# First keys of an attention kernel loaded in two pieces a head and transposed in two pieces

## The chip, the cores and the metric

The kernel runs on one core of a Trainium2 chip. The metric is the time of one execution on the device, in microseconds (us), as a median of several runs. The core has five engines, each with an instruction queue of its own that runs in order: PE (TensorE, matmuls and transposes; PEld is its loading of weights), DVE (VectorE), ACT (ScalarE), POOL (GpSimd) and SP (SyncE, which here only issues transfers). Transfers between the chip's memory (HBM) and the core's (SBUF) are issued by SP, ACT or POOL and carried by 16 DMA engines. Matmul results land in PSUM, from which DVE or ACT copy them.

## The reference

Causal attention with 16 extra "beacon" keys and values ahead of each head's own, then a two-layer network with a leaky ReLU on the joined heads. B = 8 batches, H = 8 heads, S = 576 positions, head size D = 64, 16 beacons; 4608 tokens of width 512, inner width 2048. All inputs and the output are float32.

```python
k_all = np.concatenate([beacon_k, k], axis=2)
v_all = np.concatenate([beacon_v, v], axis=2)
scores = scale * np.matmul(q, k_all.transpose(0, 1, 3, 2))
scores = np.where(causal, -1000000000.0, scores)      # beacons are never masked
a = softmax(scores)
attn_out = np.matmul(a, v_all)
x = attn_out.transpose(0, 2, 1, 3).reshape(B * S, H * D)
h = x @ w_in
out = np.maximum(0.01 * h, h) @ w_out
```

## The kernel before

**Tiling.** Heads are worked on in pairs: group g is batch g // 4, pair g % 4, so there are 32 groups. The two heads of a pair lie on partitions 0 to 63 and 64 to 127 of a transposed operand (head size on partitions, positions in columns). Keys of a group stand in `kT`: 16 beacon columns, then 576 keys. `score(g, n)` (s0.0 to s0.3 for group 0) multiplies blocks of 128 key columns with the queries: s0.0 uses key columns 0 to 127 (beacons and keys 0 to 111), s0.1 the next 128, s0.2 and s0.3 the rest. Each is followed by an exponential on ACT (L276) into `aT`, and POOL masks the triangles (`mask`, L289). `value(g, half)` multiplies the masked exponentials with V (L359). After that `up` and `down` steps do the two layers (L442, L544), which fill PE for the rest of the run.

**How a position lies in a loaded tile.** A load of queries or keys is read as "(p i) d": row p of 64 partitions holds the nine consecutive positions 9p to 9p + 8, so that a row of float32 is 9 x 64 x 4 = 2304 bytes. PE transposes one i of the nine at a time, and the copy out of PSUM puts position 9p + i into column 9p + i.

**Loads.** Queries and keys of the first eight groups are loaded by POOL with a cast to bfloat16 (`load_qk`, L158); V by POOL too (`load_v_cast`, L209 and L214). The keys of group 0 alone go by SP without a cast (`load_first_keys`, L163): two transfers, one a head, each of 64 rows to partitions 0 to 63 of two buffers `first_k`, which share their memory with the tiles `gsum2` (the profile calls them gsum). The beacon keys of the first two batches go by ACT's queue (L185). After the cast of head 0 on ACT (L928) and head 1 on DVE (L929) both heads stand side by side in `k_nat0`, 64 partitions.

**Transposes of group 0.** `t_q(0, 0)` transposes the queries (18 transposes, L243) and ACT copies all 576 columns out (`q0.1`: engine 1 of the pair dve, act). `t_q(0, 1)` transposes the keys from `k_nat0`, nine transposes of 64 x 128 (L238), and DVE copies them in two parts: the first 13 rows of p (117 columns) and the rest (459 columns), L249.

**Order.** The order on every engine is written out by hand. A string of steps is read by `run`: s score, m mask, v value, q and k transposes with copies, l and V loads, i loads of the first layer's weights, w and W unused matmuls that write nothing that is read, and so on. Steps without a letter in `run` (the first keys, beacon casts and transposes, the making of constants) are called between the strings. In the head this is the order:

```python
        unused(13, 256)
        cast_beacon_k(0, 2, nc.scalar.copy)
        beacon_transposes(0, 2)
        unused(13)
        nc.scalar.copy(out=k_nat0[:, :, 0], in_=first_k[0])
        nc.vector.tensor_copy(out=k_nat0[:, :, 1], in_=first_k[1])
        run("q0.1 k0 w2.384 s0.0 m0.0 w3.256 s0.1 q1 s0.2 m0.1 k1 s0.3 m0.2")
```

An engine takes from this list the instructions that are its own, in this order. POOL's queue has all loads from l0.0 to i0 ahead of the first mask.

Of the kernel before, what the change touches and what calls it, by code (L numbers as in the profile page):

```python
# [8 lines left out]
FP32 = mybir.dt.float32  # L9
BF16 = mybir.dt.bfloat16  # L10
# [5 lines left out]
def kernel(  # L16
# [11 lines left out]
    nc = tc.nc  # L28

    B, H, S, D = q.shape  # L30
    NB = beacon_k.shape[2]
# [74 lines left out]
    def sum_tile(n):  # L106
        return sumpool.tile([128, NF * 128], BF16, name=f"gsum{n}")

    QK = 2 * RI * D
    first_k = [  # L110
        sum_tile(2)[0:RP, 0:QK].bitcast(FP32).rearrange("p (i d) -> p i d", i=RI) for _ in range(2)
    ]
    k_nat0 = singles.tile([RP, RI, 2, D], BF16, name="k_nat0")
    bk_raw = singles.tile([128, B, D], FP32, name="bk_raw")
    bk = singles.tile([128, B, D], BF16, name="bk")

    def make_pads():
        nc.vector.memset(k_all[:, :, NB + S :], 0.0)
        for t in a_bufs:
            for c in PADS:  # L120
                nc.vector.memset(t[:, :, c : c + 48], 0.0)

    def make_ones():
        for t in v_bufs:
            nc.vector.memset(t[:, :, :, D : D + 1], 1.0)
# [30 lines left out]
    def load_qk(g, which):  # L156
# [2 lines left out]
            out=raw_of(b, grp)[which][rows],  # L159
            in_=(q, k)[which][b, 2 * hp : 2 * hp + 2].rearrange("h (p i) d -> p h i d", i=RI),  # L160
        )

    def load_first_keys():  # L163
        for h in range(2):
            nc.sync.dma_start(out=first_k[h], in_=k[0, h].rearrange("(p i) d -> p i d", i=RI))

    def load_natural(g, which):
        b, hp = divmod(g, NPAIR)
# [15 lines left out]
    def load_beacon_k(b0, b1, eng):  # L184
        eng.dma_start(out=bk_raw[:, b0:b1], in_=beacon_k[b0:b1].rearrange("b h n d -> (h n) b d"))  # L185

    def cast_beacon_k(b0, b1, copy):
        copy(out=bk[:, b0:b1], in_=bk_raw[:, b0:b1])

    def beacon_transposes(b0, b1):  # L190
        ps = ps_one.tile([128, 1024], BF16, name="tp", tag="one")
        for b in range(b0, b1):
            for par in range(2):
                nc.tensor.transpose(
                    ps[par * 64 : par * 64 + 64, (b - b0) * 128 : (b - b0 + 1) * 128], bk[:, b], ident
                )
        for par in range(2):
            ps_ = slice(par * 64, par * 64 + 64)
            src = ps[ps_, 0 : (b1 - b0) * 128].rearrange("p (x e n) -> p e x n", e=2, n=NB)[:, par]
            if b0 == 0:  # L200
                nc.vector.tensor_copy(out=k_all[ps_, :, 0:NB], in_=src)
            else:
                nc.vector.tensor_copy(out=bkT[ps_, b0:b1].rearrange("p b h n -> p (b h) n"), in_=src)
# [15 lines left out]
    def operand(g, which):  # L219
        qk.setdefault(g, [None, None])  # L220
        if which == 0:
            qk[g][0] = headpool.tile([128, S], BF16, name="qT", bufs=5)
            return qk[g][0]
        qk[g][1] = k_bufs[g % NK]
        return qk[g][1][:, NB : NB + S]
# [5 lines left out]
    def t_q(g, which, copy):  # L231
        b, hp, grp, rows = where(g)
        dst = operand(g, which)
        ps = ps_one.tile([128, 1024], BF16, name="tp", tag="one")
        psv = ps[:, 0:S].rearrange("c (i p) -> c i p", i=RI)
        for i in range(RI):
            if (g, which) == (0, 1):
                nc.tensor.transpose(  # L238
                    psv[:, i], k_nat0[:, i].rearrange("p h d -> p (h d)"), ident[0:RP, 0:RP]
                )  # L240
                continue
            for par in range(2):
                nc.tensor.transpose(  # L243
                    psv[par * 64 : par * 64 + 64, i], qk_raw[b, grp][which][rows, par, i], ident[rows, rows]
                )
        cut = 13 if (g, which) == (0, 1) else RP
        for lo, hi, eng in ((0, cut, copy), (cut, RP, nc.vector.tensor_copy)):
            if lo < hi:
                eng(  # L249
                    out=dst.rearrange("c (p i) -> c p i", i=RI)[:, lo:hi],  # L250
                    in_=psv.rearrange("c i p -> c p i")[:, lo:hi],
                )

    probs = {}

# [206 lines left out]
    def weight_sums(part):  # L462
        b11, b12 = w_out_sb[:, 0:HF, 0:HD], w_out_sb[:, 0:HF, HD:DM]
        b21, b22 = w_out_sb[:, HF:NF, 0:HD], w_out_sb[:, HF:NF, HD:DM]
        t1, t2, t4 = (w_sum[:, i] for i in range(3))
        tt = nc.vector.tensor_tensor
        if part == 0:
            tt(out=t1, in0=b12, in1=b11, op=SUB)
            tt(out=t2, in0=b22, in1=t1, op=SUB)
            tt(out=t4, in0=b21, in1=t2, op=SUB)  # L470
        else:
            tt(out=b12, in0=b22, in1=b12, op=SUB)
# [348 lines left out]
    def unused(n, cols=128):  # L821
        ps = ps_one.tile([128, 512], FP32, name="av", tag="one")
        r, w = max(1, cols // 128), min(cols, 128)
        for i in range(n):
            nc.tensor.matmul(
                out=ps[:, 0 : r * w].rearrange("p (r w) -> p r w", w=w),
                lhsT=blank,
                rhs=blank[:, None, 0:w].to_broadcast([128, r, w]),
                start=True,
                stop=True,  # L830
            )

    def unused_ahead(g, half, n):
        if (g, half) not in avs:
            avs[g, half] = ps_one.tile([128, 512], FP32, name="av", tag="one")
        for i in range(n):
            nc.tensor.matmul(
                out=avs[g, half][:, 400:512], lhsT=blank, rhs=blank[:, 0:112], start=True, stop=True
            )

    NG = B * NPAIR
    KEPT, LEAD, LEFT = 4, 4, 14

# [16 lines left out]
    def run(steps):  # L860
        for step in steps.split():
            op, a = step[0], [int(x) for x in step[1:].split(".")] if step[1:] else []
            if op == "s":
                score(*a)
            elif op == "m":
                mask(*a)
            elif op == "v":
                value(*a)
            elif op == "e":
                value_ahead(*a)  # L870
            elif op == "x":
                finish(*a)
            elif op == "l":
                load_qk(*a)
            elif op == "V":
                load_v_cast(*a)
            elif op == "N":
                load_natural(*a)
            elif op == "T":
                turn_pair(a[0])  # L880
            elif op == "y":
                x_turn(a[0])
            elif op == "q" or op == "k":
                t_q(a[0], 0 if op == "q" else 1, (dve, act)[a[1] if len(a) > 1 else 0])
            elif op == "b":
                beacon_columns(a[0], (dve, act, pool)[a[1]])
            elif op == "u":
                up()
            elif op == "d":
                down()  # L890
            elif op == "w":
                unused(*a)
            elif op == "W":
                unused_ahead(*a)
            elif op == "i":
                load_w_in(a[0])
            elif op == "o":
                load_w_out(a[0])
            elif op == "t":
                weight_sums(a[0])  # L900
            else:
                raise ValueError(step)

# [8 lines left out]
        }  # L912
    )
    with order:
        load_first_keys()
        load_beacon_k(0, 2, nc.scalar)
        nc.vector.memset(blank, 0.0)
        nc.vector.memset(ident, 0.0)
        run("l0.0 l1.0")
        make_identity(nc, ident, nomemset=True)  # L920
        make_ones()
        run("l1.1 l2.0 l2.1 V0.0 V0.1 l3.0 l3.1 V0.2 V0.3 V0.4 l4.0 l4.1 i0")
        make_pads()
        unused(13, 256)
        cast_beacon_k(0, 2, nc.scalar.copy)
        beacon_transposes(0, 2)
        unused(13)
        nc.scalar.copy(out=k_nat0[:, :, 0], in_=first_k[0])  # L928
        nc.vector.tensor_copy(out=k_nat0[:, :, 1], in_=first_k[1])  # L929
        run("q0.1 k0 w2.384 s0.0 m0.0 w3.256 s0.1 q1 s0.2 m0.1 k1 s0.3 m0.2")  # L930
        run("w2.384 s1.0 m1.0 q2 s1.1 k2 w2.384 s1.2 m1.1 w2.384 s1.3 m1.2 W0.0.4 s2.0 m2.0 W0.0.4 s2.1 W0.0.6 q3 l5.0 l5.1 s2.2 k3 w4.384 v0.0 m2.1 s2.3 i1 m2.2 W0.1.4 s3.0 m3.0 v1.0 s3.1 v0.1 s3.2 v1.1 m3.1 l6.0 l6.1 s3.3 x0.1 m3.2")
        run("v2.0 V1.0 V1.1 q4 v2.1 x1 k4.1 v3.0 v3.1 x2.1 s4.0 s4.1 x3 m4.0 V1.2 V1.3 V1.4 l7.0 l7.1 u u s4.2 s4.3 q5 k5 m4.1 m4.2 u o0 u")
        load_beacon_k(2, B, nc.gpsimd)
        run("s5.0 s5.1 m5.0 u u u s5.2 s5.3 q6 k6 m5.1 m5.2 o1 u u s6.0 s6.1 m6.0 u v4.0 u v4.1 y4 N8.0 N8.1 u s6.2 s6.3 q7 k7 m6.1 m6.2 u")
        cast_beacon_k(2, B, nc.gpsimd.tensor_copy)
        run("u v5.0 u v5.1 N9.0 s7.0 s7.1 m7.0 d x5 v6.0 v6.1 T8 d s7.2 s7.3")
        beacon_transposes(2, B)
        run("m7.1 m7.2 N9.1 u b8.2 b9.2 b10.2 b11.2 x6 v7.0 T9 v7.1 d d d N10.0 N10.1 d V2.0 V2.1 x7 t0 T10")


        FIRST = 2 * NPAIR
        COLS = FLAT[NKB]
# [99 lines left out]
```

## Time and profile before

| | us |
|---|---|
| median of the runs | 324.58 |
| lowest and highest run | 324.3, 325.61 |
| span of the profiled execution | 323.8 |
| PE busy in the span | 314.3 |
| ACT busy | 203.8 |
| POOL busy | 184.3 |
| DVE busy | 168.0 |

The span is the time from the first to the last instruction of one profiled execution; of that execution no other time is given. A row of the timeline reads: start in us, length in us, engine, line of the kernel, operation, what is written and read, shapes, how many instructions were merged, and in brackets how long the engine stood idle before and which instruction or transfer ended that. A row of the groups has the count, the total busy time in us, the mean in ns and the idle time. A row of the stretches has the stretch, its length, and the busy time of PE, PEld, DVE, ACT and POOL. A row of the DMA queues has packets, MB and the time that the packets took as a share of all 16 engines over the stretch; queue 0 is POOL's, queue 1 SP's, queue 10 ACT's.

### The profile page before, as it was taken

The numbers are of one execution on the slowest core, as the hardware profiler recorded it, in microseconds if no ns is written. First come the engines' busy times: TensorE is split into PE (matmuls) and PEld (weight loads), VectorE is DVE, ScalarE is ACT, GpSimd is POOL, SyncE is SP. The second block draws the span as 40 slices with busy tenths as digits, with TensorE's granted clock in tenths as the row PEclk, the third lists the DMA queues.
The fourth block names the chain that finished last, engine by engine and source line by source line (L and its number), as shares of the span: only waits on it lengthen the run. The fifth ranks groups of instructions, "written<-read, shape, count | busy, mean of one in ns | idle before, by whom it ended". The sixth has DMA issues, their size and how long they took to land.

```text
span 323.8 us, 8701 instructions
## 1 busy us (share of the span) xinstructions
PE 314.3 (97%) x3468; PEld 219.1 (68%) x3494; DVE 168.0 (52%) x341; ACT 203.8 (63%) x346; POOL 184.3 (57%) x354
## 2 busy tenths in 40 slices
PE   7999999999999999999999999999999999999995
PEld 4575555444588557855788888656875697688784
DVE  3464245508255244444443454525464689577954
ACT  4968962387855786478746874687458547455510
POOL 8895868999996787659875977666221000000000
PEclk9999999999999999999999999999999999999999
DMA  8999999999999999999999999999222100200123
GB/s 137 129 189 192 124 214 140 169 177 188 135 152 160 216 138 129 114 186 97 141 176 174 99 143 119 188 128 129 44 81 82 26 2 32 75 25 2 65 67 130
DMA packets 155256, 39.78 MB, mean 123 GB/s; under 512 B 142368, under 2 KB 152480, under 8 KB 155216
## 3 DMA queue, kind: packets, MB, share of 16 engines
q0 software_dynamic: 99824, 18.54, 91.1%
q1 hardware_dynamic: 55120, 20.62, 38.3%
q8 instruction: 27, 0.44, 0.6%
q14 instruction: 13, 0.11, 0.1%
q10 hardware_dynamic: 272, 0.07, 0.1%
HBM read 37.22 MB, written 9.44 MB: 144 GB/s over the span
## 4 chain that ended last, share of the span: by engine, by line
PE 72%; DMA 14%; POOL 9%; ACT 3%; issue 1%; DVE 0%; POOLq 0%; ACTq 0%; SPq 0%
PE acc L442 24%; PE acc L544 19%; PE sc L544 11%; PE av L359 6%; PE sc L314 5%; PE acc L663 5%; DMA w_out_sb<-in_moe_w_out_dram 4%; DMA gsum<-in_k_dram 4%; POOL aT L289 3%; DMA k_nat<-in_k_dram 3%; DMA v_aug<-in_v_dram 2%; ACT aT L333 2%; DMA kT<-k_nat 2%; POOL gsum L158 1%; POOL v_aug L214 1%
## 5 line engine op out<-in xcount | busy, mean ns | idle before, releaser
L442 PE MATMUL acc<-xT,w_in_sb 128*128 128x512 bf16 (+1 forms) x537 | 116.5, 354 | 1.5 <-ACT aT L329 0.3
L450 ACT ACTIVATE gT<-acc 128x512 bf16<-128x512 f32 x124 | 70.8, 623 | 33.1 <-PE acc L442 32.6
L289 POOL TENSOR_SCALAR_AFFINE_SELECT aT<-aT 128x256 bf16<-128x256 bf16 (+2 forms) x160 | 59.7, 403 | 51.4 <-ACT aT L329 31.5
L442 PEld LDWEIGHTS <-w_in_sb 128*128 128x128 bf16 x560 | 51.7, 98 | 43.9 <-issue 2.9
L544 PEld LDWEIGHTS <-gT 128*128 128x128 bf16 x512 | 48.7, 98 | 7.7 <-issue 1.8
L333 ACT ACTIVATE aT<-sc 128x1024 bf16<-128x1024 f32 (+3 forms) x64 | 51.7, 892 | 0.0
L329 ACT ACTIVATE aT<-sc 128x512 bf16<-128x512 f32 (+3 forms) x64 | 29.0, 520 | 27.8 <-PE sc L314 27.8
L388 DVE RECIPROCAL rec<-av 128x6 f32<-128x6 f32 (+1 forms) x64 | 12.0, 187 | 65.0 <-PE av L359 64.4
L359 PEld LDWEIGHTS <-aT 128*128 128x128 bf16 (+1 forms) x960 | 36.9, 98 | 9.2 <-issue 1.4
L544 PEld LDWEIGHTS <-gsum 128*128 128x128 bf16 x384 | 36.5, 98 | 6.5 <-issue 0.4
L359 PE MATMUL av<-v_aug,aT 128*128 128x65 bf16 (+1 forms) x960 | 39.8, 194 | 0.8 <-DMA v_aug<-in_v_dram 0.4
L214 POOL DMA_DIRECT2D v_aug<-in_v_dram x40 | 34.1, 856 | 4.2 <-DMA w_in_sb<-in_moe_w_in_dram 3.8
L171 POOL DMA_DIRECT2D k_nat<-in_k_dram x48 | 34.8, 730 | 0.9 <-DMA w_out_sb<-in_moe_w_out_dram 0.3
L171 POOL DMA_DIRECT2D q_nat<-in_q_dram x48 | 34.8, 729 | 0.6 <-issue 0.4
L389 DVE TENSOR_TENSOR x_nat<-av,rec 128x384 bf16<-128x384 f32 (+1 forms) x64 | 31.4, 491 | 2.2
L544 PE MATMUL acc<-w_out_sb,gT 128*128 128x256 bf16 x240 | 28.9, 273 | 0.4 <-ACT gT L450 0.4
L276 ACT ACTIVATE aT<-sc 128x1024 bf16<-128x1024 f32 (+3 forms) x32 | 26.0, 874 | 4.7 <-PE sc L267 2.5
L314 PE MATMUL sc<-qT,kT 64*128 64x80 bf16 (+22 forms) x384 | 22.2, 250 | 0.3
L314 PEld LDWEIGHTS <-kT 64*128 64x128 bf16 x384 | 12.8, 94 | 11.2 <-issue 7.6
L544 PE MATMUL acc<-w_sum,gsum 128*128 128x256 bf16 x160 | 20.1, 273 | 0.0
L575 ACT COPY p<-acc 128x512 f32<-128x512 f32 x15 | 9.1, 604 | 16.8 <-PE acc L544 16.8
L785 DVE TENSOR_TENSOR gsum<-gT 128x1024 bf16<-128x1024 bf16 x16 | 11.0, 688 | 15.7 <-ACT gT L450 15.7
(95 smaller groups left out, 339.0 us busy)
## 6 DMA issues: line engine op xcount, KB each, us to landing
out_dram<-p SPq DMA_DIRECT2D x26, 256.0 KB, 3.2
q_nat<-in_q_dram POOLq DMA_DIRECT2D x48, 72.0 KB, 5.5
k_nat<-in_k_dram POOLq DMA_DIRECT2D x48, 72.0 KB, 5.3
v_aug<-in_v_dram POOLq DMA_DIRECT2D x24, 128.0 KB, 6.5
w_in_sb<-in_moe_w_in_dram POOLq DMA_DIRECT2D x2, 1024.0 KB, 12.4
w_out_sb<-in_moe_w_out_dram POOLq DMA_DIRECT2D x2, 1024.0 KB, 12.1
out_dram<-u SPq DMA_DIRECT2D x8, 256.0 KB, 2.7
gsum<-in_q_dram POOLq DMA_DIRECT2D x8, 144.0 KB, 7.1
```

The lines of the kernel that those rows point to most:

```text
L171: nc.gpsimd.dma_start(out=t[:, :, par], in_=(q, k)[which][b, 2 * hp + par].rearrange("(t p) d -> p t d", p=NR),)
L214: nc.gpsimd.dma_start(out=dst[lo : ROWS[c], c, :, 0:D], in_=v[b, :, OFF[c] : OFF[c] + n].rearrange("h p d -> p h d"),)
L276: nc.scalar.activation(out=aT[:, :, c0 : c0 + w], in_=sc[:, :, 0:w], func=AF.Exp, scale=0.125)
L289: nc.gpsimd.affine_select(out=view, in_=view, compare_op=ALU.is_ge, fill=0.0, base=128 - n if lo == 0 else 0, channel_multiplier=-1, patte ...
L314: nc.tensor.matmul(out=(sc[par] if apart else sc[:, par])[:, at : at + b - a], lhsT=kT[ps_, c * 128 : (c + 1) * 128], rhs=qT[ps_, q0 : q0 ...
L329: nc.scalar.activation(out=probs[g][:, par, lo:hi], in_=sc[par][:, at : at + hi - lo], func=AF.Exp, scale=0.125)
L333: nc.scalar.activation(out=probs[g][:, :, lo:hi], in_=sc[:, :, at : at + hi - lo], func=AF.Exp, scale=0.125)
L359: nc.tensor.matmul(out=avv[:, n, 0 : D + 1], lhsT=aT[0 : ROWS[c], par, a0 : a0 + 128], rhs=va[0 : ROWS[c], c, 2 * hp + par, :], start=(c = ...
L389: nc.vector.tensor_tensor(out=x_nat[:, t0:t1].rearrange("p t e d -> p (t e) d"), in0=avv[:, :, 0:D], in1=rec[:, n0:n1, None].to_broadcast( ...
L442: nc.tensor.matmul(out=acc[:, lo:hi], lhsT=w_in_cols(fc, j), rhs=xT[:, j, x0 : x0 + hi - lo], start=(j == 0), stop=(j == NJ - 1), skip_gro ...
L450: nc.scalar.activation(out=gT[i][:, fc, :], in_=acc, func=AF.Prelu, alpha=0.01)
L544: nc.tensor.matmul(out=acc[:, lo : lo + HD], lhsT=left(i, n, fc, tile), rhs=right(n, fc), start=(lo == 0 and fc == 0), stop=(fc == HF - 1) ...
```

## The change

The two heads' first keys now lie one below the other, head h on partitions 64h to 64h + 63 of one buffer `first_k`, and each head comes in two transfers on SP: rows 0 to 26 of p (keys 0 to 242), then rows 27 to 63. The order on SP is: both heads' first pieces (F0.0, F1.0), then both second pieces (F0.1, F1.1). The first pieces are cast by ACT (h0.1) and DVE (h1.0). `first_keys(0)` (g0.0) makes 18 transposes of 27 partitions each, and DVE copies 243 columns. After the scores s0.0 and s0.1, `first_keys(1)` (g1.0) makes 18 transposes of 64 partitions, and DVE copies the other 333 columns. Ahead of it H0, on DVE, casts the whole of `first_k`, 128 partitions x 576, into `k_nat0` at once; on DVE's queue it stands behind its part of the first queries' copy.

The copy of the first queries (q0.1) is split: ACT copies rows 0 to 31 of p (288 columns), DVE the other 288. The cast h1.0 stands on DVE ahead of the copies of the beacon transposes. There are 8 and 4 unused matmuls of 128 columns around g0.0 where there were 13 ahead of the casts. The rest of the order is as before; all of it is now one string, `HEAD`, with letters for what was called between the strings.

```diff
-    first_k = [
-        sum_tile(2)[0:RP, 0:QK].bitcast(FP32).rearrange("p (i d) -> p i d", i=RI) for _ in range(2)
-    ]
-    k_nat0 = singles.tile([RP, RI, 2, D], BF16, name="k_nat0")
+    first_k = sum_tile(2)[:, 0:QK].bitcast(FP32).rearrange("p (i d) -> p i d", i=RI)
+    k_nat0 = singles.tile([128, RI, D], BF16, name="k_nat0")
+    PIECES = (0, 27, RP)
...
-    def load_first_keys():
-        for h in range(2):
-            nc.sync.dma_start(out=first_k[h], in_=k[0, h].rearrange("(p i) d -> p i d", i=RI))
...
-            if (g, which) == (0, 1):
-                nc.tensor.transpose(
-                    psv[:, i], k_nat0[:, i].rearrange("p h d -> p (h d)"), ident[0:RP, 0:RP]
-                )
-                continue
...
-        cut = 13 if (g, which) == (0, 1) else RP
-        for lo, hi, eng in ((0, cut, copy), (cut, RP, nc.vector.tensor_copy)):
...
+        cuts = (0, 32, RP) if g == 0 else (0, RP)
+        for lo, hi, eng in zip(cuts, cuts[1:], (copy, nc.vector.tensor_copy)):
...
+    def load_first_keys(h, piece):
+        lo, hi = PIECES[piece : piece + 2]
+        nc.sync.dma_start(
+            out=first_k[h * 64 + lo : h * 64 + hi], in_=k[0, h].rearrange("(p i) d -> p i d", i=RI)[lo:hi]
+        )
+
+    def cast_first_keys(h, copy):
+        rows = slice(h * 64, h * 64 + PIECES[1])
+        copy(out=k_nat0[rows], in_=first_k[rows])
+
+    def first_keys(piece, copy):
+        if piece == 0:
+            operand(0, 1)
+        dst = qk[0][1][:, NB : NB + S].rearrange("c (p i) -> c p i", i=RI)
+        lo, hi = PIECES[piece : piece + 2]
+        ps = ps_one.tile([128, 1024], BF16, name="tp", tag="one")
+        psv = ps[:, 0 : RI * RP].rearrange("c (i p) -> c i p", i=RI)
+        for i in range(RI):
+            for h in range(2):
+                rows = slice(h * 64, h * 64 + hi)
+                nc.tensor.transpose(psv[h * 64 : h * 64 + 64, i, 0:hi], k_nat0[rows, i], ident[rows, rows])
+        copy(out=dst[:, lo:hi], in_=psv.rearrange("c i p -> c p i")[:, lo:hi])
...
+            elif op == "H":
+                (dve, act)[a[0]](out=k_nat0, in_=first_k)
```

The head of the new order:

```
F0.0 F1.0 K Z I F0.1 F1.1 l0.0 l1.0 J O l1.1 l2.0 l2.1 V0.0 V0.1 l3.0 l3.1 V0.2 V0.3 V0.4 l4.0 l4.1 i0 P
w13.256 C h0.1 h1.0 B w8 g0.0 w4 q0.1 H0 s0.0 m0.0 s0.1 w3.256 g1.0 q1 s0.2 m0.1 k1 s0.3 m0.2 w2.384 s1.0
...
```

K, Z, I, J, O and P are the beacon keys' load and the making of constants as before; C and B are the beacon keys' cast and transposes.

More of the change, by code (lines that the diff above doesn't have):

```diff
@@ L245, in t_q @@
                 )
-        cut = 13 if (g, which) == (0, 1) else RP
-        for lo, hi, eng in ((0, cut, copy), (cut, RP, nc.vector.tensor_copy)):
[L248 to L252, printed above, removed]
+        cuts = (0, 32, RP) if g == 0 else (0, RP)
+        for lo, hi, eng in zip(cuts, cuts[1:], (copy, nc.vector.tensor_copy)):
+            eng(
+                out=dst.rearrange("c (p i) -> c p i", i=RI)[:, lo:hi],
+                in_=psv.rearrange("c i p -> c p i")[:, lo:hi],
+            )
[3 more added lines that the diff above has]
+            out=first_k[h * 64 + lo : h * 64 + hi], in_=k[0, h].rearrange("(p i) d -> p i d", i=RI)[lo:hi]
+        )
+    def cast_first_keys(h, copy):
[13 more added lines that the diff above has]
+        copy(out=dst[:, lo:hi], in_=psv.rearrange("c i p -> c p i")[:, lo:hi])
     probs = {}
@@ L839, in unused_ahead @@
             )
+    HEAD = "F0.0 F1.0 K Z I F0.1 F1.1 l0.0 l1.0 J O l1.1 l2.0 l2.1 V0.0 V0.1 l3.0 l3.1 V0.2 V0.3 V0.4 l4.0 l4.1 i0 P w13.256 C h0.1 h1.0 B w8 g0.0 w4 q0.1 H0 s0.0 m0.0 s0.1 w3.256 g1.0 q1 s0.2 m0.1 k1 s0.3 m0.2 w2.384 s1.0 m1.0 q2 s1.1 k2 w2.384 s1.2 m1.1 w2.384 s1.3 m1.2 W0.0.4 s2.0 m2.0 W0.0.4 s2.1 W0.0.6 q3 l5.0 l5.1 s2.2 k3 w4.384 v0.0 m2.1 s2.3 i1 m2.2 W0.1.4 s3.0 m3.0 v1.0 s3.1 v0.1 s3.2 v1.1 m3.1 l6.0 l6.1 s3.3 x0.1 m3.2 v2.0 V1.0 V1.1 q4 v2.1 x1 k4.1 v3.0 v3.1 x2.1 s4.0 s4.1 x3 m4.0 V1.2 V1.3 V1.4 l7.0 l7.1 u u s4.2 s4.3 q5 k5 m4.1 m4.2 u o0 u L s5.0 s5.1 m5.0 u u u s5.2 s5.3 q6 k6 m5.1 m5.2 o1 u u s6.0 s6.1 m6.0 u v4.0 u v4.1 y4 N8.0 N8.1 u s6.2 s6.3 q7 k7 m6.1 m6.2 u c u v5.0 u v5.1 N9.0 s7.0 s7.1 m7.0 d x5 v6.0 v6.1 T8 d s7.2 s7.3 D m7.1 m7.2 N9.1 u b8.2 b9.2 b10.2 b11.2 x6 v7.0 T9 v7.1 d d d N10.0 N10.1 d V2.0 V2.1 x7 t0 T10"
     NG = B * NPAIR
@@ L900, in run @@
                 weight_sums(a[0])
+            elif op == "F":
+                load_first_keys(*a)
+            elif op == "K":
+                load_beacon_k(0, 2, nc.scalar)
+            elif op == "Z":
+                nc.vector.memset(blank, 0.0)
+            elif op == "I":
+                nc.vector.memset(ident, 0.0)
+            elif op == "J":
+                make_identity(nc, ident, nomemset=True)
+            elif op == "O":
+                make_ones()
+            elif op == "P":
+                make_pads()
+            elif op == "C":
+                cast_beacon_k(0, 2, nc.scalar.copy)
+            elif op == "B":
+                beacon_transposes(0, 2)
+            elif op == "h":
+                cast_first_keys(a[0], (dve, act)[a[1]])
+            elif op == "H":
+                (dve, act)[a[0]](out=k_nat0, in_=first_k)
+            elif op == "g":
+                first_keys(a[0], (dve, act)[a[1]])
+            elif op == "L":
+                load_beacon_k(2, B, nc.gpsimd)
+            elif op == "c":
+                cast_beacon_k(2, B, nc.gpsimd.tensor_copy)
+            elif op == "D":
+                beacon_transposes(2, B)
             else:
@@ L914 @@
     with order:
[L915 to L938, printed above, removed]
+        run(HEAD)
         FIRST = 2 * NPAIR
```

## The prediction

> **What bounds the kernel now.** I read the page first, then the busy time by stretch, then the head (the first 24 us, where the change lies) engine by engine in the timeline, and last the DMA view of short windows.
>
> ```profile
> span 323.8 us, 8701 instructions
> PE 314.3 (97%) x3468; PEld 219.1 (68%) x3494; DVE 168.0 (52%) x341; ACT 203.8 (63%) x346; POOL 184.3 (57%) x354
> ```
> ```profile
> 20.00:78.00 58.00, 56.05 (x684) 30.90 (x693) 26.45 (x55) 37.98 (x62) 48.42 (x92) 1.00 1.93 171
> ...
> 78.00:150.00 72.00, 71.27 (x781) 48.16 (x785) 33.45 (x69) 50.52 (x88) 56.41 (x108) 1.00 1.72 151
> 150.00:257.00 107.00, 106.43 (x1193) 77.49 (x1199) 52.09 (x108) 71.69 (x127) 62.19 (x120) 1.00 1.33 121
> ```
>
> The second fence gives length and then PE's busy time. From 20 to 257 us PE idles 1.95, 0.73 and 0.57 us (length less busy time); its queue runs in order. So a delay of PE at 20 us reaches the end almost whole, and a gain there does too, if nothing holds PE before 20 us. What holds it in the head:
>
> ```profile
> 6.42 0.64 ACT L249 COPY qT<-tp 128x576 bf16<-128x576 bf16 x1 [1.98 <-PE tp L243]
> 7.74 8.89 ACT L276 ACTIVATE aT<-sc 128x1024 bf16<-128x1024 f32 x11 [0.68 <-PE sc L267]
> 17.66 2.48 ACT L276 ACTIVATE aT<-sc 128x576 bf16<-128x576 f32 x3 [1.02 <-PE sc L267]
> 20.56 1.54 ACT L276 ACTIVATE aT<-sc 128x832 bf16<-128x832 f32 x2 [0.42 <-PE sc L267]
> ```
> ```profile
> L276 ACT ACTIVATE aT<-sc 128x1024 bf16<-128x1024 f32 x4 | 4.1, 1024 | 0.7 <-PE sc L267 0.7
> L276 ACT ACTIVATE aT<-sc 128x928 bf16<-128x928 f32 x4 | 3.7, 937 | 0.0
> ```
> ```profile
> 5.91 0.47 PE L243 MATMUL tp<-ident,gsum 64*64 64x64 bf16 x18 [0.83 <-DMA gsum<-in_q_dram]
> ...
> 7.31 0.39 PE L267 MATMUL sc<-qT,kT 64*128 64x512 bf16 x2
> ...
> 8.82 0.35 PE L267 MATMUL sc<-qT,kT 64*128 64x336 bf16 x4
> ...
> 17.32 0.30 PE L267 MATMUL sc<-qT,kT 64*128 64x208 bf16 x4
> ...
> 19.89 0.35 PE L359 MATMUL av<-v_aug,aT 80*128 80x65 bf16 x6 [0.39 <-DMA v_aug<-in_v_dram]
> ```
>
> ACT runs eleven exponentials without a pause from 7.74 to 16.63 us, then waits 1.02 for score s2.3 (17.32 on PE, behind the values v0.0), and 0.42 later. At 19.89 PE waits for a load of V. So the first scores set ACT's pace up to 16.6 us; the loads of V, with 1.44 us of ACT's idling behind them, set PE's place at 20 us.
>
> **The change part by part.** Before, s0.0 waits for these: the two casts of the first keys, the nine transposes and a copy of 117 columns.
>
> ```profile
> 4.29 0.46 DVE L201 COPY kT<-tp 64x128 bf16<-64x128 bf16 x2 [2.21 <-PE tp L194]
> 5.62 0.74 DVE L929 CAST k_nat<-gsum 64x576 bf16<-64x576 f32 x1 [0.87 <-DMA gsum<-in_k_dram]
> 6.97 0.82 DVE L249 COPY kT<-tp 128x117 bf16<-128x117 bf16 x2 [0.60 <-PE tp L238]
> ```
> ```profile
> L249 DVE COPY kT<-tp 128x459 bf16<-128x459 bf16 x1 | 0.6, 625 | 0.0
> ...
> L249 DVE COPY kT<-tp 128x117 bf16<-128x117 bf16 x1 | 0.3, 283 | 0.6 <-PE tp L238 0.6
> ```
>
> *First piece and queries.* The copies give about 1 ns a column: 243 columns 0.41, 288 columns 0.45, 333 columns 0.50 us. The query transposes end at 6.38, both half copies at 6.42 + 0.45 = 6.87 instead of 7.06 (ACT) and 7.25 (first keys on DVE), so s0.0 starts at 6.9 instead of 7.31: 0.4 us earlier. This holds if DVE is free by then. Its queue now has cast h1.0 ahead of the two beacon copies (0.46), then the 243-column copy. Its transfer is issued at 1.39 as before; by the landings below it comes between 4.3 and 5.6, the cast (0.74) ends between 5.0 and 6.3, the copies between 5.9 and 7.2, and the query half between 6.87 and 7.65. I take 6.9, since 27 rows are fewer than 64. The nine transposes and 0.82 us of copies that go are replaced by 36 transposes (0.47 for 18), half of them while PE waits for the queries, half beside ACT's first exponentials. Fewer unused matmuls (8 and 4 for 13) cost nothing: PE waits for the queries there.
>
> *Second piece.* It holds 37 partitions a head, is issued third and fourth on SP, and one cast, H0, waits for both. Behind H0 stand on DVE the copies of the second piece, of q1, k1 and all later ones; on PE, behind the transposes g1.0, stand q1, s0.2 and everything after; on ACT the third exponential; on POOL the mask m0.2 and, behind it, the loads of group 5. H0 is the added wait, and its price is the landing.
>
> ```profile
> L165 SPq DMA_DIRECT2D gsum<-in_k_dram x2: 571/574/576, 0.8 to 1.4; - x2
> ...
> DMA to landing us min/median/max: 2.9/3.5/4.2
> ```
> ```profile
> q1 hardware_dynamic: 80, 0.15, 43.1%
> q0 software_dynamic: 24, 0.03, 30.5%
> ```
> ```profile
> q0 software_dynamic: 267, 0.28, 83.0%
> q1 hardware_dynamic: 80, 0.15, 24.2%
> ```
> ```profile
> q0 software_dynamic: 2104, 0.44, 235.9%
> ```
> ```profile
> q10 hardware_dynamic: 272, 0.07, 0.1%
> ```
>
> The first DMA fence is the issue of the first keys; the next two are the windows 2.0 to 3.2 and 3.2 to 5.3 us, one transfer of queue 1 in each (packets, MB, share of 16 engines); then 7 to 10 us; then the page's row of the beacon keys. A transfer of 64 rows is 80 packets and one of 256 rows 272: the rows and 16 end marks, one for each engine, so 4 and 16 rows to each. A row took 0.242 x 16 x 2.1 / 64 = 0.127 us of its engine, a packet of queue 0 beside it 0.830 x 33.6 / 267 = 0.104.
>
> Row counts of 27 and 37 do not divide by 16, and no row of before shows what is done with a remainder. Ends: two or three rows to each engine (nothing lost), or equal shares alone: 27 on nine engines by three, 37, a prime, on one. I take equal shares, because equal shares are all that the rows show, and that both transfers begin at the same engine, as each shows a full set of 16. Then 74 rows stand in one engine's line. All but the rows of a landing is 2.9 - 4 x 0.127 = 2.4 us, and the third issue is at 0.81 + 2 x 0.574 = 1.96, so the last row lands at 4.36 + 74 x 0.127 = 13.8 us with the engine to itself, and with a queue-0 packet in turn after each row 74 x 0.104 = 7.7 later, 21.5. Queue 0 has work throughout, but from 7 us on in small packets (209 bytes on average, 1.05 KB before), so I take 17.0.
>
> The sum: 17.0, H0 0.74 (L929 has the same width), 18 transposes 0.47, the copy 0.50, so s0.2 starts at 18.8 against 8.82: **10.0 us late**. ACT then runs through: its idle 1.02 + 0.42 goes, 8.5 us are left at 22 us. From 20 to 78 us PE has 1.95 us of idling; POOL's loads slip along with the masks, so I let 1.5 of it be regained: **7.0 us**. The span becomes 330.8. The profiled execution is known by its span alone; the median of the runs shown, 324.58, lies 0.8 above it, so the forecast is 331.6 us. The 0.4 us gain of the first score is lost in this wait. V on the loaded engine comes up to 72 x 0.127 = 9.1 us late, PE reaches it 8.5 late: hidden but for 0.6 us, in the range.
>
> [...]
>
> *The idle PE.* In that wait PE stands still from about 8 to 17.7 us.
>
> ```profile
> 1.07 2.95 PE L825 MATMUL av<-blank 128*128 128x256 bf16 x13 [1.07 <-DVE blank L917]
> ...
> 4.18 0.90 PE L825 MATMUL av<-blank 128*128 128x128 bf16 x13
> ```
>
> The first 13 unused matmuls take 227 ns for 256 columns, the later ones 69 for 128, a rate 1.6 times higher. If PE falls back to the first rate for 3 us, it loses 1.1 us; ACT, the slower there, covers it. I take 0; 1.1 more stays within the range below. [...]
>
> **The rivals.** (A) *Even dealing* (the other side, not slower). The last transfer is issued at 2.53 and lands 4.2 later at 6.7; H0 starts when DVE is free at 6.9, ends at 7.6, transposes 8.1, copy 8.6, s0.2 at 8.7. Its exponential is due at 7.34 + 1.02 + 0.94 = 9.3, so ACT runs on, 0.4 us earlier than before, until it waits for s2.3 behind the loads of V as now, only longer. Time 324.5. For it: 37 rows over 16 engines is the natural split, and the bytes are the same. Against: no remainder is seen anywhere. It decides while the second piece lands by about 10.4 us: s0.2 is then 3.4 late, what ACT's 1.44 and PE's 1.95 us take up. (B) *Equal shares, but each head on an engine of its own*: 37 rows land at 2.53 + 2.4 + 4.7 = 9.6, or 13.5 in turns; s0.2 is 2.6 to 6.5 late; halfway it is 4.5, less 1.44 and 1.5 regained 1.6: 326.1 us, between 324.5 and 329.6. Against it speaks that nothing shows a transfer starting elsewhere than the one before. (C) *Even dealing, and the early score carries through*: 0.4 us to the end, 324.2, if nothing held PE at 20 us; the 0.39 us wait at 19.89 speaks against it.
>
> **How the numbers follow.** Equal shares have 0.75, of which one engine 0.68 and B 0.07, as nothing but equal shares is seen; A has 0.19, C 0.03, and a gain over 0.5%, for which I find no mechanism, 0.03. About 0.5% (1.6 us) is what a measurement here can tell from no change. Slower: 0.68 and half of B, 0.71; same: A, C and the rest of B, 0.26; faster 0.03. One engine alone spans 328.0 (13.8 us: s0.2 6.8 late, less 1.44 and 1.95, 3.4) to 337.7 (21.5 us: 14.5 late, less 1.44, 13.1). A, C and B together hold more than 2 in 10, so the range reaches down to them: 324.0 to 338.0; the forecast's own range is 328 to 338.
>
> **What would show it.** Right: H0 (now a cast of 128x576) starts near 17 us with a DMA named as its releaser; ACT has two exponentials, a pause of some 9 us, then the rest in one run; packets of queue 1 trickle over 10 us instead of two bursts. Wrong: H0 near 7 us, nine or more exponentials in a run, PE's wait at 19.89 longer than 0.39 (A). If H0 waits and the end does not move by over 3 us, the step "a delay of PE reaches the end" fails.

## The result, and the profile after

The changed kernel takes 336.21 us (median of 4 runs, 334.9 to 339.13) against 324.44 us before (4 runs): ratio 1.0364, 95% interval 1.0326 to 1.0402, so 11.8 us slower, inside the range of 324 to 338 and on the side forecast; the forecast gave 7.0 of the 11.8 us. The profiled execution is the fastest of the four: 334.9 us, with a span of 333.2. Single runs of most kernels here, the one before too, take 4 to 5 us longer than the rest, and the ratios leave most of those out, so a ratio and the medians beside it can differ.

First the page of the changed kernel, then ACT, DVE and PE of its head from the timeline, and last one row of PE in the kernel before.

```profile
span 333.2 us, 8754 instructions
PE 319.0 (96%) x3492; PEld 221.2 (66%) x3518; DVE 168.3 (51%) x343; ACT 204.1 (61%) x346; POOL 184.6 (55%) x354
```
```profile
10.72 1.86 ACT L288 ACTIVATE aT<-sc 128x1024 bf16<-128x1024 f32 x2 [1.19 <-PE sc L279]
17.79 1.62 ACT L288 ACTIVATE aT<-sc 128x832 bf16<-128x832 f32 x2 [5.22 <-PE sc L279]
20.06 2.06 ACT L288 ACTIVATE aT<-sc 128x1024 bf16<-128x1024 f32 x2 [0.65 <-PE sc L279]
23.01 0.86 ACT L288 ACTIVATE aT<-sc 128x832 bf16<-128x832 f32 x1 [0.89 <-PE sc L279]
24.12 0.65 ACT L288 ACTIVATE aT<-sc 128x576 bf16<-128x576 f32 x1 [0.24 <-PE sc L279]
25.14 1.93 ACT L288 ACTIVATE aT<-sc 128x1024 bf16<-128x1024 f32 x2 [0.38 <-PE sc L279]
27.49 0.86 ACT L288 ACTIVATE aT<-sc 128x832 bf16<-128x832 f32 x1 [0.41 <-PE sc L279]
29.24 3.89 ACT L288 ACTIVATE aT<-sc 128x576 bf16<-128x576 f32 x5 [0.89 <-PE sc L279]
```
```profile
15.41 0.46 DVE L935 CAST k_nat<-gsum 128x576 bf16<-128x576 f32 x1 [5.40 <-DMA gsum<-in_k_dram]
```
```profile
8.39 0.69 PE L233 MATMUL tp<-ident,gsum 64*64 64x64 bf16 x18 [1.92 <-DMA gsum<-in_q_dram]
10.07 1.00 PE L279 MATMUL sc<-qT,kT 64*128 64x512 bf16 x4 [0.99 <-DVE qT L238]
...
17.22 0.53 PE L279 MATMUL sc<-qT,kT 64*128 64x336 bf16 x4
...
22.90 0.82 PE L837 MATMUL av<-blank 128*128 128x384 bf16 x2
...
28.90 0.30 PE L279 MATMUL sc<-qT,kT 64*128 64x208 bf16 x4
```
```profile
9.88 0.50 PE L825 MATMUL av<-blank 128*128 128x384 bf16 x2
```

H0 (L935) waits for the first keys until 15.41 us; two exponentials have run by then, and the third comes 5.22 us after them. Two things more are to be seen. The first queries come at 8.39 instead of 5.91 us, so s0.0 is not early but late (10.07 instead of 7.31). And PE is slow, ahead of the wait and behind it: two unused matmuls of 384 columns take 0.82 us where they took 0.50 before, 18 transposes 0.69 instead of 0.47 (the queries' at 8.39 already), and ACT pauses five times for PE between 17.8 and 28.4 us (0.65 + 0.89 + 0.24 + 0.38 + 0.41 = 2.57). From s0.2 (17.22, 8.4 us late) to s2.3 (28.90, 11.6 late) the delay grows by 3.2 us; at the end of the span 9.4 are left. (The ratio's 11.8 us is over all four runs; this profile is of the fastest.)

The DMA view of two windows of the changed kernel, 1.7 to 3.1 and 3.1 to 15 us, the row of queue 1 from each (packets, MB, share of 16 engines):

```profile
q1 hardware_dynamic: 73, 0.13, 31.5%
```
```profile
q1 hardware_dynamic: 75, 0.17, 4.4%
```

Together 148 packets, where two transfers of 64 rows were 160: the 128 rows and 20 end marks instead of 32, which is 9 + 9 + 1 + 1: of the marks' packets 18 stand between 2.21 and 2.95 us, one at 7.78 and one at 14.70. The 74 rows of the second pieces take 0.044 x 16 x 11.9 = 8.4 us of engine time within 11.9, and in the trace each starts as the one before ends (to 4 ns) or later, from 2.95 to 14.60 us: one row after the other, as on one engine.

POOL's loads have 16 end marks each, and the trace has their times; here the 15th and the last, in us:

```
              before           changed
load          15th   16th      15th   16th
q of group 0   5.66   5.87      5.24   8.35
q of group 1   6.21   6.57      5.99  10.49
k of group 1   7.76   7.84      7.25  12.03
q of group 2   8.88   9.18      8.88  13.67
V block 1     12.98  13.14     12.75  16.95
```

Fifteen marks are on time in the changed kernel; the last is 3 to 5 us behind them, and a load is there when the last one is: the transposes of the first queries start at 8.39, behind the mark at 8.35. That only one mark of 16 is late is read as the rows of both heads on the same engine, which has a part of POOL's loads too; they landed one head after the other, at 8.16 and 15.29 us. POOL's waits end with such landings: its third load of V is issued at 12.32 us, 0.29 behind the mark at 12.03, instead of 8.13.

### The profile page after: what moved, and what is told of

It reads as the page before. It is cut to its first block, busy times and chain, and to the rows that moved or that the text cites. A ratio compares the mean times of both kernels' runs of the same rounds, so it can differ in the third digit from the quotient of the medians.

```text
span 333.2 us, 8754 instructions
## 1 busy us (share of the span) xinstructions
PE 319.0 (96%) x3492; PEld 221.2 (66%) x3518; DVE 168.3 (51%) x343; ACT 204.1 (61%) x346; POOL 184.6 (55%) x354
## 4 chain that ended last, share of the span: by engine, by line
PE 85%; DMA 8%; ACT 3%; POOL 1%; issue 1%; DVE 0%; SPq 0%; ACTq 0%; DVEq 0%
PE acc L454 29%; PE acc L556 19%; PE sc L556 11%; PE av L371 9%; PE sc L326 6%; PE acc L675 5%; DMA gsum<-in_k_dram 4%; PE sc L279 3%; DMA kT<-k_nat 3%; ACT aT L345 2%; PE tp L233 2%; DMA k_nat<-in_k_dram 2%; PE acc L531 1%; PE av L837 1%; POOL k_nat L166 1%
## 5 line engine op out<-in xcount | busy, mean ns | idle before, releaser
L288 ACT ACTIVATE aT<-sc 128x1024 bf16<-128x1024 f32 (+3 forms) x32 | 26.6, 875 | 12.1 <-PE sc L279 11.9
L797 DVE TENSOR_TENSOR gsum<-gT 128x1024 bf16<-128x1024 bf16 x16 | 11.2, 703 | 16.5 <-ACT gT L462 16.4
## 6 DMA issues: line engine op xcount, KB each, us to landing
w_in_sb<-in_moe_w_in_dram POOLq DMA_DIRECT2D x2, 1024.0 KB, 10.5
```

The costliest lines, as they stand in the source:

```text
L288: nc.scalar.activation(out=aT[:, :, c0 : c0 + w], in_=sc[:, :, 0:w], func=AF.Exp, scale=0.125)
```

## The experiments

The theory after the result: the 37 rows go through one engine, and the late landing, PE's loss of rate and the late loads of POOL all follow from that. The rivals: the new order is slow in itself (the cast H0 behind the queries' copy, twice the transposes, four issues on SP); or only the wait counts, or only the contention; or PE's rate costs nothing because ACT sets the pace, as the prediction had it.

### The cut at 32 rows

```diff
-    PIECES = (0, 27, RP)
+    PIECES = (0, 32, RP)
```

> The changed kernel with the cut at 32 rows of 64 instead of 27, so that each of the four transfers has 32 rows, two to each engine; all else as in the changed kernel. One engine (37 rows stood in one engine's line): four bursts of queue 1 with 16 end marks each, H0 starts at about 7 us, ten or more exponentials in one run, 324 to 325 us. Order (the one cast H0 behind the queries' copy, twice the transposes and four issues on SP are slow themselves): the pause of ACT after two exponentials stays, at least 5 us of it, and the time stays over 331 us.

Measured: 326.01 us median, ratio to the kernel before 0.9996 (0.9953 to 1.0038). The rows of queue 1 (window 0 to 16 us), ACT and DVE in its profile:

```profile
q1 hardware_dynamic: 192, 0.30, 6.6%
```
```profile
7.40 3.35 ACT L288 ACTIVATE aT<-sc 128x1024 bf16<-128x1024 f32 x4 [0.97 <-PE sc L279]
10.99 5.78 ACT L288 ACTIVATE aT<-sc 128x1024 bf16<-128x1024 f32 x7 [0.24 <-PE sc L279]
17.61 3.89 ACT L288 ACTIVATE aT<-sc 128x576 bf16<-128x576 f32 x5 [0.84 <-PE sc L279]
```
```profile
6.95 0.46 DVE L935 CAST k_nat<-gsum 128x576 bf16<-128x576 f32 x1
```

192 packets are 128 rows and 4 x 16 marks; H0 starts at 6.95 without a wait. The median is 1 to 2 us over what was expected, as that of the kernel before was in the same series (325.54). Five rows moved from one piece to the other take away all of the loss: the order is not slow in itself. The run of exponentials has one pause of 0.24 us, which the expectation did not have. It starts at 7.40 instead of 7.74, and ACT is at 17.61 where it was at 17.66: the lead of 0.34 us is gone there, and the time is that of before. What takes the lead is PE's own work: from 10.6 us on it has no wait, and it reaches the score s2.3 at 17.27 where it was at 17.32.

```profile
17.27 0.30 PE L279 MATMUL sc<-qT,kT 64*128 64x208 bf16 x4
```

### The cut at 28 rows

```diff
-    PIECES = (0, 27, RP)
+    PIECES = (0, 28, RP)
```

> The cut at 28 rows, so transfers of 28 and 36 rows, no multiples of 16. If the dealing is in equal shares by the largest divisor up to 16, 28 rows go to 14 engines and 36 to 12, queue 1 shows 2 x 14 + 2 x 12 = 52 end marks beside 128 rows (180 packets), H0 starts at about 7 us and the time is that of the cut at 32 within 0.5%. If any count that isn't a multiple of 16 falls to one engine, or to few, H0 starts at 13 us or later and the time is over 331 us.

Measured: ratio 1.0026 (0.9956 to 1.0095), median 328.79 us; eight of the ten runs took over 328 us, two 324.2 and 324.7.

```profile
q1 hardware_dynamic: 180, 0.30, 8.2%
```
```profile
8.05 0.48 DVE L935 CAST k_nat<-gsum 128x576 bf16<-128x576 f32 x1
```
```profile
12.47 0.82 PE L837 MATMUL av<-blank 128*128 128x384 bf16 x2
```

180 packets are 52 marks, as 2 x 14 + 2 x 12 gives. So the largest divisor up to 16 fits the marks of this cut and of those at 27 and 32 (20 and 64), and 28 and 36 rows, no multiples of 16, did not fall to one engine. H0 is at 8.05 and not 7, behind the queries' half copy; PE ran at its lower rate in this profile too (0.82 us for two matmuls of 384 columns), from the start to 20 us at least, though nothing made it wait over 1.0 us there once it had begun. The loss of the landing is gone, but that the time is within 0.5% of the cut at 32 is not shown: the medians are 0.9% apart, and why this cut ran at the lower rate was not tried.

### 27 rows and 37 in two transfers

```diff
     PIECES = (0, 27, RP)
+    CUTS = ((0, 27), (27, 59), (59, RP))
...
-        lo, hi = PIECES[piece : piece + 2]
+        lo, hi = CUTS[piece]
...
-F0.1 F1.1 l0.0
+F0.1 F1.1 F0.2 F1.2 l0.0
```

> The changed kernel with its first piece of 27 rows kept and the other 37 rows of a head in two transfers, 32 and 5, six transfers on SP in all. Equal shares by the largest divisor up to 16: end marks 9 + 9 + 16 + 16 + 5 + 5 = 60, so 188 packets of queue 1, H0 at 7 to 8 us, the time within 1% of before. If the piece of 27 rows (or any rest) is what hurts, H0 stays over 12 us and the time over 331 us.

Measured: ratio 1.0113 (1.0055 to 1.0171), 328.96 us.

```profile
q1 hardware_dynamic: 188, 0.30, 8.2%
```
```profile
7.61 0.46 DVE L936 CAST k_nat<-gsum 128x576 bf16<-128x576 f32 x1
```
```profile
7.70:24.60 16.90, 16.77 (x205) 8.51 (x204) 6.01 (x10) 9.94 (x12) 11.56 (x23) 0.50 1.67 161
```

The marks are as expected (60) and H0 is at 7.61: the piece of 27 rows does no harm by its landing. The time is a little above the 1% expected. The last row is the stretch from 7.7 to 24.6 us, with the granted clock third from the end: 0.50, although PE is busy 16.77 of 16.90 us. So this version lost PE's rate in its profile; whether anything else in it costs time is open.

### The wait without the load on one engine

Cut at 32; the second pieces are issued on ACT's queue, written behind its second exponential. In the trace the issues run from 7.50 to 8.32 us, while the first exponential is at work.

```diff
-w4 q0.1 H0 s0.0 m0.0 s0.1 w3.256 g1.0
+w4 q0.1 s0.0 m0.0 s0.1 F0.1.1 F1.1.1 H0 w3.256 g1.0
```

> The cut at 32 rows, but the second pieces are issued by ACT behind its second exponential, at about 9.3 us, so they land late (about 12.5 to 13.5 us) while no engine carries more than its share: the wait without the load on one engine. Wait: H0 at 12.5 to 13.5, s0.2 at 14.2 to 15.2 (5.4 to 6.4 late), POOL's transfers on time (first queries by 6 us, V as before), the end 3 to 5 us late where PE's rate holds, 327.5 to 329.5, up to 332 with PE at half rate after the pause. If contention was all of the loss: under 326 us.

Measured: ratio 1.0315 (1.0266 to 1.0365), 335.13 us, more than expected.

```profile
14.32 0.46 DVE L935 CAST k_nat<-gsum 128x576 bf16<-128x576 f32 x1 [7.51 <-DMA gsum<-in_k_dram]
```
```profile
8.00:10.60 2.60, 0.00 (x0) 0.00 (x0) 0.00 (x0) 1.15 (x2) 2.38 (x4) 1.00 2.74 135
10.60:24.20 13.60, 9.29 (x126) 4.56 (x126) 3.95 (x6) 5.19 (x7) 5.72 (x14) 0.50 1.28 129
24.40:30.00 5.60, 5.60 (x115) 3.81 (x115) 3.22 (x8) 4.70 (x7) 4.07 (x9) 1.00 0.82 119
```

The rows landed at 14.2 instead of 12.5 to 13.5 us: the transfers took 6.0 us (median) from issue to landing, beside POOL's transfers, where the first pieces took 2.2. POOL's early loads are on time here: PE takes up the first queries at 5.41 us without a wait, and from issue to landing queries, keys and V take 4.3, 5.8 and 7.0 us (medians; 5.7, 6.7 and 8.1 in the cut at 32). So the wait, with what it does to PE's rate, suffices for a loss of nearly the changed kernel's size. The stretches show the rate: PE has nothing to do from 7.9 to 14.8 us, its granted clock falls to 0.50 at 10.6 and is back at 1.00 only at 24.3, 9.5 us after PE took up work again.

### The load on one engine without the wait

Cut at 32, and two transfers of 37 rows each behind the four, into memory that nobody reads.

```diff
-F0.1 F1.1 l0.0
+F0.1 F1.1 E0 E1 l0.0
```

> The cut at 32 rows, and two more transfers of 37 rows each on SP behind the four, into memory that nobody reads: the load on one engine without anybody waiting for these rows. Wait (the loss is H0's waiting for the rows): H0 at about 7 us, 324 to 326 us. Contention (POOL's transfers lose their turns on that engine, so queries, keys and V come late whoever waits for the rows): the first queries come at over 7.5 us instead of 5.9, V 2 us late or more, and the time is 327 to 332 us.

Measured: ratio 1.0133 (1.0069 to 1.0198), 330.38 us.

```profile
7.02 0.46 DVE L943 CAST k_nat<-gsum 128x576 bf16<-128x576 f32 x1
```
```profile
11.29 0.69 PE L234 MATMUL tp<-ident,gsum 64*64 64x64 bf16 x18 [1.91 <-DMA gsum<-in_k_dram]
```
```profile
11.20:24.80 13.60, 13.51 (x158) 6.99 (x158) 4.36 (x7) 7.18 (x9) 8.63 (x18) 0.50 0.93 102
```

H0 is on time; PE waits for the keys of group 1 instead, until 11.29; in the kernel before they had landed by 7.84. The first queries were in time (PE's transposes of them start at 5.59 us without a wait), which was not expected: the extra transfers are issued fifth and sixth. So contention without a wait for these rows costs 4 to 5 us, with an interval wholly above 1; and again PE's clock falls, at 11.2 us, so part of this is PE's rate. The 4.8 us here and the 10.1 of the wait (medians) add up to more than the 11.8 of the change: each holds a loss of PE's rate, and they can't be added.

### PE's pauses filled with unused matmuls

Three versions of the changed kernel, cut at 27. They differ in the unused matmuls ahead of the query transposes, ahead of s0.0, and ahead of the second key transposes.

```diff
-g0.0 w4 q0.1 H0 s0.0 m0.0 s0.1 w3.256 g1.0
+g0.0 w14 q0.1 H0 s0.0 m0.0 s0.1 w24.256 g1.0
```

> The changed kernel with 31 more unused matmuls in PE's two waits (14 for 4 ahead of the query transposes, 24 for 3 of 256 columns ahead of the second key transposes), cut at 27 as changed. Clock (PE's matmuls ran at about half rate to 26.7 us, and ACT waited for them): PE is at its full rate at 17 us, transposes of 18 take 0.47 instead of 0.69, ACT's pauses after s0.2 shrink by 2 us or more and the time falls by 2 to 4 us, to 332 to 334. Landing alone (PE's rate costs nothing since ACT sets the pace): within 1 us of the changed kernel, 335 to 337.

Measured: 334.59 us, ratio 1.0228 (1.0133 to 1.0323); single runs from 331.28 to 340.32. The median lies between the two expectations, so the time decides nothing. In its profile (333.78 us) PE has the full rate from about 13 us on (its 24 unused matmuls from 10.58 us on take 4.09 us, where all at the first 13's 227 ns would take 5.4; 18 transposes behind them take 0.47), and of ACT's five pauses behind s0.2 two are left:

```profile
19.46 5.78 ACT L288 ACTIVATE aT<-sc 128x1024 bf16<-128x1024 f32 x7 [0.24 <-PE sc L279]
26.07 3.89 ACT L288 ACTIVATE aT<-sc 128x576 bf16<-128x576 f32 x5 [0.84 <-PE sc L279]
```

The second version fills all three pauses:

```diff
-g0.0 w4 q0.1 H0 s0.0 m0.0 s0.1 w3.256 g1.0
+g0.0 w22 q0.1 H0 w9 s0.0 m0.0 s0.1 w38.256 g1.0
```

> The changed kernel, cut at 27, with all three of PE's pauses filled by unused matmuls (22 for 4 ahead of the query transposes, 9 ahead of s0.0, 38 for 3 of 256 columns ahead of the second key transposes): the landing of the 37 rows without the loss of PE's rate. Landing plus clock: the granted clock is 1.0 from about 7 us on and stays there, H0 still at 15 to 16 us, s0.2 at 17.0 to 17.8, ACT runs the nine exponentials behind it with one short pause at most, and the time is 329.5 to 332.5 us, 4 to 6 below the changed kernel. Landing alone: 334 to 337 us as the changed kernel.

Measured: 334.49 us, ratio 1.0235 (1.0181 to 1.029). A miss: in its profile (334.9 us) the matmuls ended at 13.8 us, a pause of 3.3 us was left ahead of the second key transposes, and the clock fell between 15.8 and 15.9. Two runs reached 330.86 and 331.09, two took 340.73 and 340.86.

```profile
17.07 0.53 PE L263 MATMUL tp<-ident,k_nat 64*64 64x64 bf16 x12 [3.32 <-DVE k_nat L935]
```
```profile
15.90:26.00 10.10, 8.80 (x122) 4.25 (x122) 3.97 (x6) 5.00 (x6) 4.87 (x12) 0.50 0.82 108
```

The third has 58 of these matmuls:

```diff
-g0.0 w4 q0.1 H0 s0.0 m0.0 s0.1 w3.256 g1.0
+g0.0 w22 q0.1 H0 w9 s0.0 m0.0 s0.1 w58.256 g1.0
```

> As the filled version of the changed kernel, with 58 unused matmuls instead of 38 ahead of the second key transposes, so that PE's last pause before H0, 3.3 us there, shrinks to about 1.2 us. Clock: the granted clock stays at 1.0 through 30 us in the profile, s0.2 stands at 17.0 to 18.0, ACT's nine exponentials behind it have no pause over 0.4 us but the one ahead of s2.3, and the median is 330 to 332 us. If the rate is lost at half the runs again, or the matmuls run at half rate and hold PE back (58 x 0.21 = 12.4 us), single runs reach 338 to 342 and the median stays at 334 or above.

Measured: 332.52 us, ratio 1.022 (1.0188 to 1.0252), an interval wholly under that of the changed kernel; one of six runs took 339.48.

```profile
18.82 1.41 ACT L288 ACTIVATE aT<-sc 128x832 bf16<-128x832 f32 x2 [6.14 <-PE sc L279]
20.47 5.78 ACT L288 ACTIVATE aT<-sc 128x1024 bf16<-128x1024 f32 x7 [0.24 <-PE sc L279]
27.09 3.89 ACT L288 ACTIVATE aT<-sc 128x576 bf16<-128x576 f32 x5 [0.84 <-PE sc L279]
```
```profile
15.63 0.46 DVE L935 CAST k_nat<-gsum 128x576 bf16<-128x576 f32 x1 [5.28 <-DMA gsum<-in_k_dram]
```
```profile
18.00:30.00 12.00, 11.49 (x225) 6.98 (x221) 6.81 (x13) 10.10 (x13) 9.88 (x23) 1.00 0.99 150
```

H0 waits as long as in the changed kernel, and s0.2 is later still (18.43, since the 58 matmuls run on to 17.36 and hold PE 1.3 us past H0). Yet ACT's nine exponentials behind it run with one pause of 0.24 us, and the clock stays at 1.00. The median is 0.5 us over the range expected, s0.2 0.4 us. So 1.0364 - 1.022 = 1.4%, 4 to 5 us, of the loss is put down to PE's rate (with both intervals 3 to 6 us; the profiled executions are 2.5 us apart, 333.2 and 330.7). The rest, 2.2% or 7 us, is the landing with the late loads, and up to 1.2 us that the 58 matmuls themselves hold s0.2 back (18.43 for 17.22). The ratios of the three filled versions (1.0228, 1.0235, 1.022) lie within each other's intervals, although PE lost its rate in the profile of the second; so that a lower rate makes ACT pause is shown, and its price is known only roughly.

### Controls, and the change with its piece mended

The kernel before with the split of the queries' copy alone, the kernel before with more unused matmuls where PE paused for 0.83 us, and the cut at 32 with nine more ahead of s0.0:

```diff
-        cut = 13 if (g, which) == (0, 1) else RP
+        cut = {(0, 0): 32, (0, 1): 13}.get((g, which), RP)
```

> The kernel before with one part of the change alone: the first queries' copy on ACT (288 columns) and DVE (288). First keys as before. Prediction's rows: the query copy ends at 6.9 instead of 7.06 but the first keys' copy, now behind the half copy on DVE, ends at about 7.3 to 7.4 instead of 7.25, so s0.0 stays at 7.3 within 0.15 us; time within 0.5% of before. If the split were worth the first score's whole lead, s0.0 would start at 6.9 or sooner.

Measured: 324.95 us, ratio 0.999 (0.9967 to 1.0014). The split is worth nothing here. The start of s0.0 could not be compared: in the profile of this version (329.5 us) PE ran at its lower rate up to 18 us at least, although it has no wait there once it has begun at 1.07.

```profile
7.02 0.82 PE L825 MATMUL av<-blank 128*128 128x384 bf16 x2
```

```diff
-        unused(13)
+        unused(22)
```

> The kernel before with 22 for 13 unused matmuls of 128 columns ahead of the first query transposes, where PE stood idle for 0.83 us: the control for the filled versions. If unused matmuls help by themselves only where PE's rate would be lost, its median is within 0.3% of the kernel before, or below it by up to 0.5%; if they delay the queries' transposes (9 x 0.07 = 0.6 us at full rate, under the pause of 0.83; 1.2 at half rate, over it), it is up to 0.1% above.

Measured: 325.53 us, ratio 1.0014 (0.9985 to 1.0043): more unused matmuls brought nothing that can be measured in the kernel before, whose profile has the full rate from 4.2 us on (13 unused matmuls of 128 columns in 0.90 us, 1.57 in the profile of the split version).

```diff
-q0.1 H0 s0.0
+q0.1 H0 w9 s0.0
```

> The cut at 32 rows with nine more unused matmuls between the query transposes and s0.0, where PE stood idle for 1 us. [...] No clock effect: median within 0.3% of the cut at 32, as many late runs.

Measured: 325.2 us, ratio 1.0014 (0.9991 to 1.0037), lowest run 323.75; the median is 0.25% below that of the cut at 32 (326.01). PE has the full rate from 6.3 us on in its profile (18 transposes in 0.47 us), and none of its 12 runs was over 327.5, but the median is not below that of the kernel before (325.02). No version here beats the kernel before by more than can be measured.

## Why the prediction was right, and where it wasn't

**One engine for 37 rows, the same for both heads: right.** 148, 180, 188 and 192 packets for four ways of cutting leave 20, 52, 60 and 64 end marks, the number of engines each time as equal shares have it, and one late mark of 16 speaks for both heads' rows on the same one.

**The landing: somewhat early of the value taken.** H0 started at 15.41, not 17.0. In the trace a row of the second pieces starts every 0.09 us up to 6.5 us and mostly every 0.19 from then on, where 0.127 alone and 0.23 in turns were taken. H0 took 0.46, not 0.74 us (its output is now contiguous in each partition, where the cast of before wrote every second block of 64; that this is the reason was not tried by itself). So s0.2 was 8.4 us late, not 10.0.

**"ACT then runs through: its idle 1.02 + 0.42 goes" and "I take 0" for PE's rate: these are the steps that failed.** The prediction had an idle PE and a lower rate after it, for 3 us, and let ACT cover it. In the profile the lower rate stands from the start to 26.7 us, so here the wait did not bring it; that a wait can take a granted rate away is shown by the late-issue version and the second filled one (1.00 to 0.50 at 10.6 and between 15.8 and 15.9 us). The 3 us were the author's estimate, and no run shows a lower rate of that length behind a wait: in these two it lasted about 13.7 and 10.2 us. At the lower rate PE, with its scores, transposes and unused matmuls, is the slower one: ACT paused five times, and by s2.3 3.2 us were added where 1.02 should have been regained. The third filled version puts this term at about 1.4%, 4 to 5 us, against 0 taken and 1.1 held in reserve.

The idle of 1.02 us was misread, too. The prediction put it down to the loads of V, but in the kernel before PE has no wait from 10.5 us until it reaches s2.3 at 17.32: ACT waits there for PE's own queue. So a late start does not give this idle back. In the third filled version, at the full rate, 0.84 us of it stays, and from s0.2 (9.6 us late) to s2.3 (26.75, 9.4 late) only 0.2 us are regained.

That 7.0 us were forecast and 2.2% (7 us) are left without PE's loss of rate is partly luck: the forecast had 10.0 late, 1.44 and 1.5 regained; this version has 9.6 late, of which its own matmuls are 1.2, then 0.2 up to s2.3 and 2.5 behind it.

**The regaining behind 20 us: near.** Where ACT ended at 22.10 us before (22 us in the sum), it ends at 33.13 in the changed kernel, 11.0 late; at the end of the span 9.4 are left: 1.6 regained, 1.5 taken.

**"s0.0 starts at 6.9": wrong in the changed kernel, right with the cut at 32** (PE's row there begins at 6.97, ACT's at 7.40 against 7.34 forecast). The prediction priced the one engine for the keys alone and for V ("hidden but for 0.6 us"); it left out that the first queries have a part on that engine, too (one of their 16 end marks is late). In the sum this lay under H0's wait, but alone, as the extra transfers show, such contention costs 4 to 5 us, PE's loss of rate included.

**The even rival** was what the cuts at 28 and 32 do, and its time (324.5 beside a kernel before of 324.58) was right within the intervals: the lead of the first score is lost before ACT reaches 17.6 us. But the loads of V are not what takes it: in the profile of the cut at 32 PE's wait for V, 0.39 us before and expected to grow, is gone, and PE, which waits for nothing from 10.6 us on, still comes to s2.3 hardly earlier (17.27 for 17.32).

## What to carry to other kernels

Before a tile is cut into pieces for an earlier start, see what the row counts do to the transfers: 27 + 37 rows went over nine engines and one (20 end marks for two heads), 32 + 32 over all sixteen (64), and that alone was worth 3.6% of the run (ratios 1.0364 and 0.9996). The slow transfers on one engine also held up others that have a share there: the first queries came 2.5 us late (8.35 for 5.87). And where PE waits, look at its rate as well as at the wait: here about 7 us are put down to the landing and 4 to 5 to the rate.

## What the hardware showed that was not expected

PE's granted clock fell in long pauses: in the second filled version in one of 3.3 us, in the late-issue version 2.7 us after PE's last matmul. It fell in shorter ones, too: in the version with extra transfers in a pause of 1.9 us, in the one with three cuts at 7.6 us with no pause over 1.0 since 1.1 us. It held over a pause of 2.0 us in the third filled version (the 18 transposes behind it take 0.47 us). So the length of one pause does not decide it in these runs.

The full rate came late: in the kernel before it was there 3.1 us after PE's start (4.18 for 1.07); in the late-issue version it came back 9.5 us after PE took up work, and in the version with extra transfers the granted clock stayed at 0.50 for 13.6 us in which PE was busy for 13.51. In the changed kernel's head PE kept to the lower rate from the start to 26.7 us, and in the split version, where PE has no wait once it has begun, to 18 us at least. Much of PE's work there is transposes and matmuls of 64 rows (in the changed kernel from 16 to 26 us 72 query and key transposes are busy for 2.9 us and 24 score matmuls for 4.2); whether that is why was not tried, and what PE must do to be granted the clock was not settled.

In the changed kernel's profile the column of the granted clock shows 1.00 up to 26.7 us, and only the durations (0.82 for 0.50) give the lower rate away.
